# A written-out order of 1442 steps replaced by another one: linear attention and a gated MLP on one NeuronCore

## The chip, the cores and the metric

The kernel runs on one core of a Trainium2 chip. The metric is the device time of one execution in microseconds, as the median of several runs; smaller is better. The core has five engines that work side by side and wait for one another by semaphores: TensorE (PE in the profile, with PEld for its weight loads), VectorE (DVE), ScalarE (ACT), GpSimd (POOL) and SyncE (SP, which here only issues DMAs).

## The reference

The inputs are q, k, v and a complex decay a = a_re + i a_im, each of 4 batches x 8 heads x 768 positions x 48 channels, and four weight matrices. The first part is a linear attention with a decaying complex state per head; the second part is a gated MLP on the 3072 tokens of 384 features that come out of it.

```python
mag = sqrt(a_re**2 + a_im**2);  scale = minimum(mag, 0.999) / (mag + 1e-6)
for t in range(768):                       # state S is complex, 48 x 48 per head
    S = a[t] * S + outer(k[t], v[t])       # a[t] scaled as above, per row of S
    y[t] = q[t] @ real(S)
x = y as 3072 tokens x 384
g, val = x @ w_gate, x @ w_val             # 384 -> 1536
ffn = (gelu(g) * val) @ w_out              # 1536 -> 384
out = x + sigmoid(x @ w_res) * ffn
```

## The kernel before

**Tiling.** The sequence is cut into 6 chunks of 128 positions. One pair of a batch and a chunk is a unit, and `SIZES` (L19) groups the 24 units into 14 passes, numbered 0 to 13: passes 0 and 1 hold one unit each, passes 2 to 11 two units each, passes 12 and 13 one each. Within a chunk the attention is computed as matrix products; from chunk to chunk a state is carried (`Gf`, `Gb`).

**Steps.** The kernel does not issue instructions directly. The functions `prepare`, `attend` and `forward` (L373, L511 and below) are called for every pass and add steps to a plan: a step has an engine, a kind and a function that issues its instructions. There are 1442 steps. In this document a step is called by its pass and kind, for example `3.feat` or `1.gv`. The kinds that matter:

- `load` (SP): 120 transfers of 192 KB, for each unit ar, ai, q, k and vf. The weights are loaded from POOL's queue (`wgv`, `wr`, `wo`).
- `ln`, `exp`, `tai`, `sq`, `lnb`, `la`, `lh`, `ll`: logarithm of the decay's magnitude, split in a high and a low half; `cumL` (PE) sums it along the chunk and `pexpE`, `pexpI` (ACT) take exponentials. `mrd` is a small DMA of the last row, `mrc` a copy after it.
- `atan`, `carry` (a DMA that adds the last chunk's phase), `th`, `tl`, `cumT` (PE), `round` (ACT), `fr`, `abs`, `sin` (ACT): the phase, its running sum and its sine and cosine.
- `qe` and `feat` (DVE or POOL): features of q and k. They are transposed either on PE (`peT`, then a copy `cpT`; passes below `PE_T` = 6, L21) or by a DMA (`dT`, SP).
- `qk`, `am`, `av`, `kv`, `U`, `Gb`, `Gf`: the attention itself; `x` copies its result out of PSUM. `x` is transposed on PE (`peX`, `cpX`; passes below `PE_X` = 3, L20) or by a DMA (`dX`, SP).
- `gv` (PE, L605): the gate and value products, 12 steps of six matmuls for a pass; `gelu` (ACT, L610), `h` (DVE, L611), `res` (PE, L620) with `tanh` (ACT), `out` (PE, L631), `ot` (DVE), `otx` (DVE or POOL) and `store` (SP).

**Order.** `ORDER` (L43 to L106) is a list of all 1442 step numbers, written out by hand or by a program that is not part of the kernel. `Plan.run` (L161) walks through it and issues each step's instructions to its engine, so each engine executes its own steps in list order. An engine stops at an instruction whose inputs are not there, and everything behind it on that engine waits too. The list also sets three other things. A buffer goes to whichever of its copies is free first in the list: 8 PSUM banks, `WD` = 21 wide buffers (L22), `WH` = 8 half-wide ones and so on. The list decides where ScalarE changes its function table: a step carries a letter L (logarithm and exponential), T (arctangent and sine) or G (gelu and tanh), and whenever the letter differs from the last one a table load is issued:

```python
            if t.act is not None and t.act != table:
                table = t.act
                load(table)
```

The table load has line L647 in the profile. And it sets the turns of POOL and DVE: POOL's computing steps and DVE's steps of the kinds in `TWO_PORTS` (L24) are chained by an added wait whenever the turn passes from one engine to the other:

```python
            if t.port:
                if last is not None and last[0] != t.eng:
                    turn(ins, last[1])
                last = (t.eng, ins)
```

**Place.** Some steps can run on more than one engine. `place(default)` (L336) looks the step's number up in the dictionary `PLACE` (L29 to L42) and otherwise takes the default that its line names, for example `place("POOL")` for `vcast`, the cast of v to bf16.

Of the kernel before, what the change touches and what calls it, by code (L numbers as in the profile page):

```python
# [29 lines left out]
    23: "POOL", 24: "POOL", 35: "POOL", 40: "DVE", 50: "DVE", 51: "DVE", 53: "ACT", 64: "ACT", 105: "POOL", 114: "ACT",  # L30
    121: "DVE", 131: "DVE", 190: "DVE", 191: "POOL", 203: "ACT", 205: "ACT", 213: "DVE", 216: "POOL", 223: "DVE", 227: "DVE",
    230: "ACT", 252: "ACT", 285: "DVE", 291: "DVE", 305: "DVE", 306: "DVE", 333: "POOL", 334: "POOL", 338: "ACT", 340: "DVE",
    353: "DVE", 356: "POOL", 363: "DVE", 366: "POOL", 367: "DVE", 422: "DVE", 435: "ACT", 438: "POOL", 456: "DVE", 460: "DVE",
    472: "POOL", 482: "POOL", 518: "DVE", 524: "DVE", 551: "ACT", 554: "POOL", 555: "POOL", 562: "DVE", 565: "POOL",
    566: "POOL", 572: "DVE", 576: "DVE", 577: "DVE", 585: "DVE", 588: "POOL", 595: "DVE", 598: "POOL", 667: "DVE", 670: "POOL",
    671: "POOL", 681: "POOL", 682: "POOL", 691: "ACT", 700: "POOL", 710: "POOL", 746: "DVE", 767: "POOL", 779: "ACT",
    783: "POOL", 794: "POOL", 801: "ACT", 803: "ACT", 822: "POOL", 878: "DVE", 891: "ACT", 894: "POOL", 895: "POOL",
    905: "POOL", 924: "POOL", 931: "DVE", 934: "POOL", 970: "DVE", 976: "DVE", 1007: "POOL", 1017: "POOL", 1025: "ACT",
    1036: "POOL", 1042: "DVE", 1045: "POOL", 1113: "DVE", 1117: "POOL", 1124: "DVE", 1137: "ACT", 1152: "DVE", 1155: "POOL",
    1196: "DVE", 1210: "DVE", 1224: "POOL", 1225: "POOL", 1232: "DVE", 1243: "DVE", 1290: "DVE", 1296: "DVE", 1316: "ACT",  # L40
    1317: "POOL", 1325: "POOL", 1388: "ACT", 1389: "POOL", 1393: "DVE", 1397: "POOL", 1402: "DVE", 1440: "DVE",
}  # L42
ORDER = [  # L43
# [636 lines left out]
```

## Time and profile before

| | before |
|---|---|
| median of 3 runs | 262.19 us (261.19 to 263.16) |
| the profiled execution's own time | 262.64 us |
| its span, first to last instruction | 260.9 us |
| granted TensorE clock, mean | 0.98 |
| PE busy | 220.1 us (84%), 2362 matmuls |
| DVE busy | 211.2 us (81%), 372 instructions |
| ACT busy | 211.6 us (81%), 353 instructions, 36 of them table loads of 46.2 us in all |
| POOL busy | 118.8 us (46%), 138 instructions |
| transfers issued by SP | 192: 120 loads, 24 stores, 48 transposes |
| bytes moved | 41.92 MB, mean 161 GB/s |

How to read it: all times come from one profiled execution. The span ends 1.7 us short of that execution's own time. A matmul's record includes the time that it spends in the pipeline, so a PE that is busy for the whole of a stretch may still have room; the spacing from the start of one step to the start of the next tells more. Since every engine executes its part of the list in list order, the n-th step of an engine in the list is the n-th one of that engine in the trace, and each of the 1442 steps has a known start and end.

### The profile page before, as it was taken

Reading aid. Unit: us, or ns where it says so; the run is one execution under the profiler, and the core shown is the slowest. Engines: PE = TensorE matmul, PEld = TensorE weight load, DVE = VectorE, ACT = ScalarE, POOL = GpSimd, SP = SyncE. Lnnn points to the kernel's source line nnn. Section 1 sums busy time; section 2 is a strip of 40 time slices with the busy share of each in tenths; the row PEclk is TensorE's granted clock in tenths of the full one; section 3 lists DMA queues with packets and bytes.
Section 4 is the critical chain, followed back from the end, with each engine's and each line's share of the span. In section 5 each row is a group of like instructions: output and inputs, shape, how many; then the busy total and the mean of one; then the engine's idle time right before and its main releaser. Section 6 shows DMA issues by size and latency. Waiting matters only on the chain. (4 is left out here: it accounts for less than half of the span.)

```text
span 260.9 us, 6202 instructions
## 1 busy us (share of the span) xinstructions
PE 220.1 (84%) x2362; PEld 169.7 (65%) x2362; DVE 211.2 (81%) x372; ACT 211.6 (81%) x353; POOL 118.8 (46%) x138
## 2 busy tenths in 40 slices
PE   0220675799999999999999989999999989999993
PEld 0000333689878767786876767877878758876881
DVE  1476979789998989988888989888999866784463
ACT  4997979999999987999799979989988756931440
POOL 4225125869850687869435467644440510122101
PEclk9999995699999999999999999999999999999999
DMA  8999999996979999698997999999999976941221
GB/s 143 187 186 205 194 191 198 183 219 103 118 126 186 178 187 225 123 184 163 196 199 158 190 188 161 193 146 174 213 170 138 204 152 135 155 80 48 79 90 60
DMA packets 170621, 41.92 MB, mean 161 GB/s; under 512 B 164064, under 2 KB 170592, under 8 KB 170592
## 3 DMA queue, kind: packets, MB, share of 16 engines
q1 hardware_dynamic: 166144, 37.63, 85.3%
q0 software_dynamic: 4448, 3.90, 10.1%
q8 instruction: 18, 0.29, 0.5%
q14 instruction: 11, 0.09, 0.2%
HBM read 31.26 MB, written 4.72 MB: 138 GB/s over the span
## 5 line engine op out<-in xcount | busy, mean ns | idle before, releaser
L611 DVE SCALAR_TENSOR_TENSOR h<-h,pb 128x512 bf16<-128x512 bf16 (+1 forms) x84 | 48.9, 604 | 12.6 <-ACT h L610 6.8
L605 PE MATMUL pb<-xT,wv 128*128 128x256 bf16 (+1 forms) x504 | 57.6, 257 | 1.1 <-DVE h L611 0.9
L605 PE MATMUL pb<-xT,wg 128*128 128x256 bf16 (+1 forms) x504 | 56.3, 257 | 1.1 <-DMA xT<-x 0.9
L631 PE MATMUL pb<-wo,h 128*128 128x384 bf16 x288 | 55.1, 326 | 0.0
L610 ACT ACTIVATE h<-pb 128x512 bf16<-128x512 f32 (+1 forms) x84 | 41.6, 547 | 13.2 <-PE pb L605 12.6
L605 PEld LDWEIGHTS <-wg 128*128 128x128 bf16 x504 | 43.2, 98 | 7.9 <-DMA xT<-x 1.6
L605 PEld LDWEIGHTS <-wv 128*128 128x128 bf16 x504 | 43.1, 98 | 7.7 <-DMA xT<-x 1.1
L647 ACT ACT_TABLE_LOAD x36 | 46.2, 1283 | 1.3 <-PEq L664 0.7
L631 PEld LDWEIGHTS <-h 128*128 128x128 bf16 x288 | 26.4, 97 | 13.9
L537 DVE TENSOR_TENSOR am<-pb,mask 128x512 bf16<-128x512 f32 x48 | 31.9, 683 | 3.2 <-PE pb L534 2.9
L368 PEld LDWEIGHTS <-mask 128*128 128x128 bf16 x96 | 9.4, 107 | 23.5 <-issue 19.6
L638 POOL TENSOR_TENSOR ot<-ot,x 128x384 f32<-128x384 f32 x13 | 11.8, 909 | 19.7 <-DVE ot L635 18.1
L534 PE MATMUL pb<-QT,KT 96*128 96x128 bf16 x192 | 17.5, 225 | 2.6 <-DVE QT L343 1.4
L567 POOL TENSOR_TENSOR Gb<-U,M 96x384 bf16<-96x384 f32 x14 | 11.6, 827 | 17.7 <-DVE ll L418 4.2
L635 DVE SCALAR_TENSOR_TENSOR ot<-sg,pb 128x384 f32<-128x384 f32 x24 | 13.1, 547 | 6.9 <-ACT x L342 3.4
L406 POOL TENSOR_TENSOR t<-t,ai 128x768 f32<-128x768 f32 (+1 forms) x8 | 12.0, 1503 | 12.7 <-ACT t L404 8.1
L342 ACT CAST x<-pb 128x384 bf16<-128x384 f32 x17 | 8.0, 475 | 11.9 <-PE pb L548 8.7
L368 PE MATMUL pb<-th,mask 128*128 128x384 f16 x24 | 9.1, 378 | 10.0 <-DVE th L343 9.7
L534 PEld LDWEIGHTS <-KT 96*128 96x128 bf16 x192 | 13.4, 100 | 6.2 <-DMA KT<-fK 2.6
L481 POOL TENSOR_TENSOR Ke<-k,Ei 128x768 bf16<-128x768 f32 (+1 forms) x6 | 9.3, 1545 | 17.7 <-ACT Ei L427 9.3
L413 DVE SCALAR_TENSOR_TENSOR la<-s,la 128x768 f32<-128x768 f32 (+1 forms) x14 | 11.6, 836 | 6.4 <-ACT s L412 4.3
L620 PE MATMUL pb<-wr,xT 128*128 128x384 bf16 x72 | 15.3, 326 | 0.9 <-DMA xT<-x 0.9
(90 smaller groups left out, 463.5 us busy)
## 6 DMA issues: line engine op xcount, KB each, us to landing
ar<-in_a_re_dram SPq DMA_DIRECT2D x24, 192.0 KB, 4.6
ai<-in_a_im_dram SPq DMA_DIRECT2D x24, 192.0 KB, 4.7
k<-in_k_dram SPq DMA_DIRECT2D x24, 192.0 KB, 4.4
q<-in_q_dram SPq DMA_DIRECT2D x24, 192.0 KB, 4.2
vf<-in_v_dram SPq DMA_DIRECT2D x24, 192.0 KB, 4.1
out_dram<-ot SPq DMA_DIRECT2D x24, 192.0 KB, 2.5
wg<-in_moe_w_gate_dram POOLq DMA_DIRECT2D x6, 192.0 KB, 5.1
wv<-in_moe_w_val_dram POOLq DMA_DIRECT2D x6, 192.0 KB, 4.9
```

The lines of the kernel that those rows point to most:

```text
L368: nc.tensor.matmul(out=bank.tile, lhsT=mask[:, 0, :], rhs=x[:, i * DM:(i + 1) * DM], start=(j == 0), stop=(j == 1))
L406: add(e1, "tai", lambda: on[e1].tensor_tensor(out=F("t"), in0=F("t"), in1=flat(T("ai"), n), op=OP.mult), [s["ai"]], [s["t"]], n)
L534: nc.tensor.matmul(out=ap.tile[:, h, :], lhsT=kT.tile[0:DD, u * H // 2 + h, :], rhs=qT.tile[0:DD, u * H // 2 + h, :], start=True, stop=True)
L537: add("DVE", "am", lambda u=u, am=am, ap=ap: nc.vector.tensor_tensor(out=am.tile[:, u * H // 2:(u + 1) * H // 2, :], in0=ap.tile, in1=mask ...
L605: nc.tensor.matmul(out=o_.tile[:, u, :], lhsT=w_[:, k_, (2 * m + u) * 128:(2 * m + u + 1) * 128], rhs=s["xT"].tile[:, k_, 0:n].rearrange(" ...
L610: add("ACT", "gelu", lambda gp=gp, hv=hv: nc.scalar.activation(out=hv(), in_=gp.tile, func=AF.Gelu), [gp], [hh], n, "G")
L611: add("DVE", "h", lambda vp=vp, hv=hv: nc.vector.scalar_tensor_tensor(out=hv(), in0=hv(), scalar=0.5, in1=vp.tile, op0=OP.mult, op1=OP.mul ...
L620: nc.tensor.matmul(out=rp.tile, lhsT=s["xT"].tile[:, k_, i, :], rhs=wr[:, k_, :], start=(k_ == 0), stop=(k_ == KF - 1))
L631: nc.tensor.matmul(out=op_.tile, lhsT=s["h2"].tile[:, k_, i * 128:(i + 1) * 128], rhs=wo[:, k_, :], start=(k_ == 0), stop=(k_ == NF - 1))
L635: add("DVE", "ot", lambda i=i, op_=op_, ot=ot: nc.vector.scalar_tensor_tensor(out=ot.tile, in0=sg[i].tile, scalar=1.0, in1=op_.tile, op0=O ...
L638: add(e8, "otx", lambda i=i, ot=ot, e8=e8: on[e8].tensor_tensor(out=ot.tile, in0=ot.tile, in1=s["x"].tile[:, i].rearrange("p h d -> p (h d ...
L647: plan.run(ORDER, lambda table: nc.scalar.preload_act_table_set(ACT_SETS[table]), lambda ins, prev: tc.add_manual_dep(ins.ins, prev.ins.na ...
```

## The change

`PLACE` and `ORDER` are replaced, and nothing else. The steps, their dependencies, the sizes and the numbers of buffers are the same. The order is another throughout, and 85 steps run on another engine: 27 go from POOL to DVE, 22 from DVE to POOL, 13 from DVE to ACT, 9 from ACT to DVE, 9 from POOL to ACT and 5 from ACT to POOL. Walked through by `Plan.run`, the old list loads ScalarE's table 36 times and the new one 33 times. POOL has 118 steps in place of 127, ACT 325 in place of 317, DVE 368 in place of 367. By kind:

| engine | steps gained (net) | steps lost (net) |
|---|---|---|
| ACT | 4 `vcast`, 2 `th`, 2 `cpT`, 2 `Mc`, 1 `abs`, 1 `cpX`, 1 `x` | 4 `sq`, 1 `mrc` |
| DVE | 4 `sq`, 3 `tl`, 2 `Gb`, 2 `Gf`, 1 `th` | 2 `cpT`, 2 `Mc`, and one each of `qe`, `tai`, `x`, `vcast`, `abs`, `mrc`, `cpX` |
| POOL | 2 `mrc`, 1 `qe`, 1 `tai` | 3 `th`, 3 `tl`, 3 `vcast`, 2 `Gb`, 2 `Gf` |

The beginning of both (the rest of the list differs in the same manner):

```diff
 PLACE = {
-    23: "POOL", 24: "POOL", 35: "POOL", 40: "DVE", 50: "DVE", 51: "DVE", 53: "ACT", 64: "ACT", 105: "POOL", 114: "ACT",
-    121: "DVE", 131: "DVE", 190: "DVE", 191: "POOL", 203: "ACT", 205: "ACT", 213: "DVE", 216: "POOL", 223: "DVE", 227: "DVE",
+    23: "POOL", 24: "POOL", 33: "DVE", 44: "POOL", 53: "ACT", 64: "ACT", 105: "DVE", 114: "ACT", 117: "POOL", 121: "DVE",
+    145: "ACT", 190: "DVE", 191: "DVE", 203: "ACT", 213: "DVE", 223: "DVE", 227: "DVE", 228: "DVE", 230: "ACT", 252: "ACT",
...
 ORDER = [
-    16, 21, 17, 22, 97, 102, 103, 23, 24, 98, 104, 34, 105, 115, 116, 178, 117, 35, 118, 25, 179, 106, 188, 26, 27, 294, 36,
-    37, 293, 107, 108, 109, 295, 411, 110, 119, 120, 38, 28, 296, 303, 304, 111, 181, 29, 189, 410, 420, 121, 180, 305, 306,
+    16, 21, 97, 102, 98, 103, 104, 22, 105, 106, 17, 23, 24, 34, 295, 115, 35, 25, 116, 36, 107, 178, 108, 37, 294, 180, 117,
+    26, 293, 303, 179, 296, 38, 304, 181, 188, 109, 27, 118, 110, 111, 305, 119, 100, 28, 306, 189, 307, 29, 2, 30, 190, 191,
...
```

In words, for the parts that come up below: in the old list `1.sq` and `2.sq` run on POOL, in the new one on DVE; `0.abs` goes from DVE to ACT. The loads of pass 1's ar and ai stand second and third in place of third and fourth, pass 1's k stands 13th in place of 25th. ScalarE's steps ahead of its first G table come in seven groups in both lists: of 4, 2, 17, 8, 16, 8 and 11 steps before, of 5, 2, 12, 7, 19, 10 and 10 after. The last `ot`, `otx` and `store` belong to pass 13 before and to pass 12 after, on DVE and SP in both.

More of the change, by code (lines that the diff above doesn't have):

```diff
@@ L29 @@
 PLACE = {
-    23: "POOL", 24: "POOL", 35: "POOL", 40: "DVE", 50: "DVE", 51: "DVE", 53: "ACT", 64: "ACT", 105: "POOL", 114: "ACT",
-    121: "DVE", 131: "DVE", 190: "DVE", 191: "POOL", 203: "ACT", 205: "ACT", 213: "DVE", 216: "POOL", 223: "DVE", 227: "DVE",
-    230: "ACT", 252: "ACT", 285: "DVE", 291: "DVE", 305: "DVE", 306: "DVE", 333: "POOL", 334: "POOL", 338: "ACT", 340: "DVE",
-    353: "DVE", 356: "POOL", 363: "DVE", 366: "POOL", 367: "DVE", 422: "DVE", 435: "ACT", 438: "POOL", 456: "DVE", 460: "DVE",
@@ L34 @@
[L34 to L38, printed above, removed]
@@ L39 @@
-    1036: "POOL", 1042: "DVE", 1045: "POOL", 1113: "DVE", 1117: "POOL", 1124: "DVE", 1137: "ACT", 1152: "DVE", 1155: "POOL",
-    1196: "DVE", 1210: "DVE", 1224: "POOL", 1225: "POOL", 1232: "DVE", 1243: "DVE", 1290: "DVE", 1296: "DVE", 1316: "ACT",
-    1317: "POOL", 1325: "POOL", 1388: "ACT", 1389: "POOL", 1393: "DVE", 1397: "POOL", 1402: "DVE", 1440: "DVE",
+    23: "POOL", 24: "POOL", 33: "DVE", 44: "POOL", 53: "ACT", 64: "ACT", 105: "DVE", 114: "ACT", 117: "POOL", 121: "DVE",
+    145: "ACT", 190: "DVE", 191: "DVE", 203: "ACT", 213: "DVE", 223: "DVE", 227: "DVE", 228: "DVE", 230: "ACT", 252: "ACT",
@@ new lines @@
+    291: "DVE", 305: "DVE", 306: "DVE", 333: "POOL", 345: "ACT", 347: "ACT", 353: "DVE", 357: "DVE", 363: "DVE", 366: "POOL",
+    408: "DVE", 422: "DVE", 423: "DVE", 438: "POOL", 446: "DVE", 456: "DVE", 460: "DVE", 469: "DVE", 472: "POOL", 482: "POOL",
+    518: "DVE", 539: "DVE", 551: "ACT", 554: "ACT", 562: "DVE", 565: "POOL", 566: "POOL", 572: "DVE", 576: "DVE", 577: "DVE",
+    579: "ACT", 588: "POOL", 595: "DVE", 598: "POOL", 670: "ACT", 671: "POOL", 681: "POOL", 682: "POOL", 689: "ACT",
@@ new lines @@
+    691: "ACT", 700: "POOL", 710: "POOL", 711: "DVE", 752: "DVE", 767: "POOL", 783: "POOL", 794: "POOL", 801: "ACT",
+    803: "ACT", 812: "POOL", 822: "POOL", 823: "DVE", 858: "DVE", 894: "ACT", 902: "DVE", 905: "POOL", 913: "ACT", 924: "POOL",
+    991: "POOL", 1003: "ACT", 1006: "POOL", 1017: "POOL", 1025: "ACT", 1042: "DVE", 1045: "POOL", 1080: "DVE", 1086: "DVE",
+    1101: "POOL", 1113: "ACT", 1116: "POOL", 1117: "POOL", 1135: "ACT", 1137: "ACT", 1146: "POOL", 1190: "DVE", 1196: "DVE",
+    1210: "DVE", 1224: "ACT", 1225: "POOL", 1235: "POOL", 1236: "POOL", 1255: "DVE", 1296: "DVE", 1325: "POOL", 1330: "DVE",
@@ L42 @@
+    1368: "DVE", 1388: "ACT", 1389: "POOL", 1393: "DVE", 1396: "POOL",
 }
 ORDER = [
[62 rows of a table removed]
[63 rows of a table added]
 ]
```

121 rows, old and new, of the table ORDER are left out of this document.

## The prediction

> **What bounds the kernel now.** I looked first at the page's slices: who is busy when.
>
> ```profile
> PE   0220675799999999999999989999999989999993
> ...
> DVE  1476979789998989988888989888999866784463
> ACT  4997979999999987999799979989988756931440
> POOL 4225125869850687869435467644440510122101
> ```
>
> Three regimes: up to about 52 us PE is half empty while ACT and DVE work; then all three are full; from about 200 us ACT and DVE thin out and only PE is full. The chain that ended last says the same of the end: from 214.65 us on it is almost only PE.
>
> ```profile
> 221.51 7.86 PE pb L605 x72
> ...
> 244.51 6.70 PE pb L605 x120
> ```
>
> These lines give PE's real pace: six matmuls, one `gv` step, take 0.655 us with two units (7.86/12) and 0.335 us with one (6.70/20). In the same way `out` takes 0.650, `res` 0.488, a `cumL` or `cumT` 0.325, `qk` 0.225, `peT` 0.448, `av` 0.406, `kv` 0.205 us from start to start. With 120 and 48 `gv`, 72 `out`, 24 `res`, 48 sums, 48 `qk`, 20 `peT`, 20 `av`, 20 `kv` and 4.5 us of small ones this is 205.2 us, the same before and after. PE's first step starts at 9.7 us, its last ends at 256.4, so it loses 256.4 - 205.2 = 51.2 us; behind it come `ot`, `otx` and the last store, 4.5 us. **So the time is 205.2 + what PE loses + 4.5.** The first `gv` starts at 52.3 us with 10.6 us of PE work done: 41.7 us are lost in the start and 9.5 after it. By 60 us 42.8 are lost, so 8.4 in the last 200 us.
>
> Next, what feeds PE. I set each engine's steps one after the other at their start-to-start times (`gelu` 0.49, `h` 0.60, `feat` 0.87 and so on), and called the rest idle. At 60 us ACT has idled 9.4 and DVE 18.7; at 200 us 21.6 and 32.9, against 49.1 for PE. So between 60 and 200 us ACT idles 12.2, DVE 14.2, PE 6.3 of 140 us: PE bounds, the other two are close. In the start it is the reverse: ACT idles 4.3 us from 20 to 60 us, PE 23.9. There ACT's list sets the pace, with waits such as these, of ACT and DVE in the first 60 us:
>
> ```profile
> ACT CS L475 <- DVE fw L471: 1.1, 1, 1.1
> ACT fr L460 <- PE pb L368: 1.0, 3, 0.5
> ACT Ei L427 <- PE pb L368: 0.8, 1, 0.8
> ...
> ACT mr L342 <- DMA mr<-E: 0.5, 1, 0.5
> ```
> ```profile
> DVE la L413 <- ACT s L412: 4.3, 2, 3.2
> ```
>
> **The change, part by part.** *Engine sums.* The costs come from rows like these, by shape:
>
> ```profile
> L647 ACT ACT_TABLE_LOAD x36 | 46.2, 1283 | 1.3 <-PEq L664 0.7
> ...
> L409 ACT ACTIVATE s<-t 128x768 f32<-128x768 f32 x7 | 5.9, 842 | 0.0
> ...
> L411 POOL TENSOR_TENSOR s<-t 128x768 f32<-128x768 f32 x2 | 2.9, 1460 | 2.0 <-DVE t L406 1.9
> ...
> L342 ACT CAST v<-vf 128x768 bf16<-128x768 f32 x2 | 1.7, 840 | 0.0
> ```
>
> Three table loads less are 3 x 1.283 = 3.85 us. ACT gets 4.66 us of steps net: four `vcast` 2.9, two `cpT` 1.8, `th` 1.65, four small kinds 1.35, four `sq` away -2.9, `mrc` -0.1. So ACT has 0.8 us *more* to do. DVE gets 3.7 us more (`sq` 3.1, `tl` 2.6, `Gb` and `Gf` 1.9, less 3.9 for the rest), POOL 9.0 less. The saved tables do not show in PE's 205.2; in the tail, where ACT is 55% idle, nothing of this counts. What counts is the start and whether PE is fed in the middle.
>
> The Trainium skill, in ScalarE: Activation LUTs, section Terms, puts a table load at about 2.7 us. By it three loads would be 8.1 us and ACT 3.4 us lighter; the row's 1283 ns decides.
>
> *Start.* ACT's own work ahead of its first G step is 46.8 us before (first `gelu` at 55.9, so 9.1 us idle) and 46.7 after. Walking the new list with the same durations and the landing times of loads of the same rank: the wait of 1.1 us for `0.abs` goes, as ACT does it itself; the 0.5 us for pass 1's `mrc` goes, as it stands later; `2.lnb` can start at 18.5 instead of 20.8, as `2.sq` no longer waits for POOL. One wait comes: `0.cpT` on ACT needs the transpose that PE has queued behind `1.kv`, and that needs pass 1's v, load 28 in place of 23 (28.2 us before, some 33 to 35 now), about 1.1 us. This gives 6.5 us of idle if every step hits its row; the old trace has some 1.7 us of small losses beyond its listed waits, so 8.2, and I take 8.0. `1.cpX` then ends at 43.9 + 0.4 + 8.0 = 52.3 us, and PE's dense part begins with `1.res` at 52.4 with 11.2 us done: 41.2 us lost, 0.5 better.
>
> DVE has 39.9 us ahead of its first `h` before (58.3 us) and **46.4** after. Its 3.2 us wait at `2.la` goes, and at that point it has idled 10.4 instead of 13.9. Then `3.th` waits about 0.8 for its carry, `am` 0.5, and `4.fr` about 1 for `4.round`, which ACT has three microseconds later in its list: 12.5 to 14 at the first `h`, 13.3 in the middle. So the first `h` comes at 59.7, when PE's list has 18.0 us ahead of it (15.9 before): PE has lost 41.7 there, against 42.8. **Sum: -1.1 us.**
>
> *Middle.* Read at equal PE positions, the new list holds 5 us more DVE work ahead from 20 us of PE work to 180 (+5.4, +5.2 at 60, +4.9 at 100, +4.2 at 180) and 1 to 3 us more of ACT's. The five are those it did in the start's idle time. DVE idles 10% of the middle either way, mostly in pieces below 1 us, so I let PE lose the same 8.4 us after 60. If that cover is gone the price is the 5 us. SP's list has each transpose within a few ranks of its old place, and its long wait for `3.x` (17.5 us, ended at 72.8 by DVE) ends some 2 us sooner. Nothing between 60 and 256 us is free for POOL's 9 us: its idle time is already half the span.
>
> *End.* The last `out` is followed by `ot` and `otx` on DVE and the store in both lists: 4.5 us again.
>
> **The sum.** 262.64 is the profiled execution's own time, 1.7 over its span and 0.45 over the median of 262.19. 262.64 - 1.1 - 0.45 = **261.1 us**. What a measurement can tell here is about 1%: 259.6 and 264.8 are the bounds of "same".
>
> **Rivals.**
> - *The start's lead is kept whole* (0.25). If no small losses come, ACT has idled 6.5 us, PE starts dense at 50.7 with 39.5 lost (-2.2), and the earlier SP queue halves PE's gaps ahead of steps that need a DMA transpose (1.05, 0.97, 1.10, 1.06 and two of 0.3, together 4.8; I take off 1.9 in place of 2.4, as not all wait for that alone): **258.1**. For it: the waits named are real; against: DVE's first `h` holds PE back to 41.
> - *DVE becomes the bound* (0.23, slower). It has 5 us more ahead of every `gv`, and PSUM banks come free only by `h`. If the 3.2 us wait at `2.la` is replaced by another (a carry, a q or k that lands late), the first `h` comes after 62 us and PE cannot catch up: up to +5, I take +4.5: **266.7**. It decides from 62 us on; at 60 or less it is off. For it: DVE is 92% busy from 60 to 200 us; against: 14.2 us idle there.
> - *Transposes come too late* (0.13). In the list `6.dX` stands straight ahead of pass 6's first `gv`, 5.7 us of PE work ahead before; `7.dT` 1.0 (7.7), `11.dT` 1.3 to 2.8 (7 to 10). They take 3.3 to 3.9 us to land, so these three could cost 3.4 + 2.7 + 2.4, less what is lost there now: about +4, **265.1**. It needs SP to issue them as late as the list stands; SP runs by its own queue, whose ranks hardly differ.
> - *PE goes into its dense part at half clock* (0.05). From 40 to 50 us the granted clock is 0.50 and a `peT` takes 0.83 us; from 50 to 55 us its mean is 0.98, so it came back at about 50.2 us, 4.2 us after PE's steps had closed up (46.0). If another pattern just ahead of the dense part puts such a 4.2 us stretch inside it, half of it is lost: +2.1, **263.2**. The Trainium skill, in TensorE: Matmul & The Clock Gate, section What's actually happening, has full clock after about 3.4 us of sustained work; the trace agrees in kind.
> - *The change is no change* is inside the forecast: 262.2.
>
> **Chances and range.** Forecast 261.1: 0.34, itself 259 to 264.8. Faster by over 1%: the first rival 0.25 and 0.03 of the forecast, 0.28. Slower: DVE 0.23, transposes 0.10, 0.02 of the forecast, 0.35. Same: 0.37. Lead and loss are both likely, so the range takes in most of the first rival and of the second: 257.2 to 267.0.
>
> **What would show it.** 33 table loads; ACT's first G step near 54.7 and not after 56; DVE's first `h` at 59 to 60.5, its wait at `2.la` below 0.5; PE's losses 41 to 42 at the first dense step and 8 to 9 after 60 us; no PE gap above 1.5 us at passes 6, 7 and 11. It is wrong if DVE idles less than 10 us between 60 and 200 us while PE loses more than 10 there, or if the start is won by 2 us or more.

## The result

| | before | changed kernel |
|---|---|---|
| median of 20 runs each, run beside one another | 261.10 us (260.01 to 263.16) | 259.99 us (257.95 to 262.01) |
| ratio of the two | | 0.9947, 95% interval 0.9923 to 0.9970 |
| the profiled execution's own time; its span | 262.64; 260.9 us | 259.86; 258.1 us |
| last PE step ends; the rest of the span | 256.4; 4.5 us | 254.0; 4.1 us |
| PE's loss at 60, 70, 140, 200 us and at the end | 42.8, 42.9, 45.8, 49.1, 51.2 us | 44.3, 45.2, 48.1, 48.4, 48.7 us |
| ScalarE's table loads | 36 | 33 |

The change is worth half a per cent, and the interval is clear of 1. The ratio compares means and leaves out one run of the changed kernel that fell in a slower state (262.01 us); the two medians alone would give 0.9957. "PE's loss" is the prediction's measure: the time up to which PE has come less the start-to-start work that it has done by then. The frame holds: 205.2 + 48.7 + 4.1 = 258.0 us is the new span, and 1.8 us more is the execution's own time. The two profiled executions differ by 2.8 us, twice what the 20 runs show, since the one of before took 1.5 us more than the median of its kernel. What is read from these two traces below therefore shows where time is lost; its sizes are those of two executions.

First the slices of the changed kernel: who is busy when, in 40 parts of the span.

```profile
PE   0132864769999999999789999999999999999993
...
DVE  2499888997999999998988989889998967866363
ACT  5899869989999999999969989999999498331440
POOL 1424145437452395948816386716105514210011
```

The three regimes are as they were: half-empty PE up to some 52 us, everything full until about 200 us, then PE alone. The chain that ended last shows the same end (columns: start, length, what):

```profile
217.47 9.17 PE pb L606 x84
...
240.11 2.01 PE pb L606 x36
```

These are 9.17/14 = 0.655 us for a `gv` step of two units and 2.01/6 = 0.335 us for one of one unit: PE's pace is exactly the old one, so all of the difference is in what PE waits for. Of the engines' groups, the changed ones read as forecast:

```profile
L648 ACT ACT_TABLE_LOAD x33 | 42.3, 1283 | 1.3 <-PEq L665 0.7
...
L410 ACT ACTIVATE s<-t 128x768 f32<-128x768 f32 x3 | 2.5, 842 | 0.0
```

Now the start, by the waits of ACT in the first 60 us and of DVE in the first 64 us (total, times, longest):

```profile
ACT KT L343 <- PE pb L504: 2.8, 3, 2.1
ACT la L404 <- DMA ar<-in_a_re_dram: 2.4, 2, 1.5
ACT s L413 <- DVE s L412: 1.4, 3, 0.9
```
```profile
DVE t L407 <- ACT t L405: 3.4, 1, 3.4
DVE th L344 <- ACT t L437: 2.6, 1, 2.6
DVE tl L455 <- POOL t L407: 1.4, 1, 1.4
...
DVE am L538 <- PE pb L535: 1.1, 1, 1.1
```

The old 3.2 us wait at `2.la` and the 1.1 us wait of ACT for `0.abs` are gone. The wait of `0.cpT` for its transpose has come, 2.1 us long, and DVE has a wait that the prediction did not have: `tl` for POOL's `t`. This is `5.tl` waiting for `6.tai`, and not for its data but for its turn. It stands in DVE's timeline right ahead of the first `h` (start, length; the bracket is the idle time before):

```profile
59.69 0.96 DVE L455 TENSOR_TENSOR tl<-t,th 128x768 bf16<-128x768 f32 x1 [1.45 <-POOL t L407]
...
62.57 0.74 DVE L612 SCALAR_TENSOR_TENSOR h<-h,pb 128x256 bf16<-128x256 bf16 x2
```

So DVE's first `h` comes at 62.57 us. It came at 58.33 us before, and 59.7 was forecast. PE's loss by 70 us is 2.3 us *larger* than before, not 1.1 smaller.

The gain is in the middle, where PE loses 48.7 - 45.2 = 3.5 us after 70 us instead of 51.2 - 42.9 = 8.3. By the table all of it comes after 140 us: between 70 and 140 us PE loses 2.9 us in both, and from there to the end 5.4 us before and 0.6 after. PE's longest waits from 75 to 256 us, of the kernel before and then of the changed one:

```profile
PE pb L534 <- DMA KT<-fK: 1.1, 3, 0.8
PE pb L503 <- DVE fQ L486: 1.0, 2, 0.6
PE pb L605 <- DMA xT<-x: 0.9, 1, 0.9
PE pb L620 <- DMA xT<-x: 0.9, 1, 0.9
PE pb L605 <- DVE h L611: 0.9, 1, 0.9
```
```profile
PE pb L535 <- DMA KT<-fK: 1.5, 1, 1.5
PE pb L606 <- DMA xT<-x: 0.6, 1, 0.6
```

`KT<-fK` and `xT<-x` are the DMA transposes `dT` and `dX`. The row that names `h` is one of them too: it is the wait of `5.gv` at 124.26 us, where that `h` had ended 1.6 us earlier and the transpose of `5.x` landed at 124.12. No row ends on ScalarE. A row counts from the end of the last matmul's record; from start to start six gaps before make 4.8 us (`5.gv` 1.05, `7.qk` 0.97, `8.gv` 1.10, `10.res` 1.06 and two of 0.3 at `11.qk`), and two are left after: `5.gv` 0.73 and `6.qk` 1.66. Also gone are the 1.3 us before `4.peT` and `5.peT` (waits for `feat`).

### The profile page after: what moved, and what is told of

Read it like the earlier page. It is cut to its first block, busy times and chain, and to the rows that moved or that the text cites. A ratio compares the mean times of both kernels' runs of the same rounds, so it can differ in the third digit from the quotient of the medians.

```text
span 258.1 us, 6191 instructions
## 1 busy us (share of the span) xinstructions
PE 219.4 (85%) x2362; PEld 171.2 (66%) x2362; DVE 214.4 (83%) x373; ACT 210.4 (82%) x358; POOL 109.7 (42%) x129
## 4 chain that ended last, share of the span: by engine, by line
PE 59%; DVE 11%; DMA 9%; issue 7%; POOL 6%; SPq 4%; ACT 2%; DVEq 0%; POOLq 0%
PE pb L606 29%; PE pb L632 15%; PE pb L621 4%; SPq L383 4%; PE pb L369 3%; DVE h L612 3%; PE pb L535 3%; DMA q<-in_q_dram 2%; POOL t L407 2%; DMA mr<-E 2%; DMA KT<-fK 2%; DMA ai<-in_a_im_dram 2%; DMA t<-fr 2%; PE pb L547 1%; PE pb L504 1%
## 5 line engine op out<-in xcount | busy, mean ns | idle before, releaser
L606 PE MATMUL pb<-xT,wg 128*128 128x256 bf16 (+1 forms) x504 | 57.0, 257 | 1.3 <-ACT sg L623 0.9
L606 PE MATMUL pb<-xT,wv 128*128 128x256 bf16 (+1 forms) x504 | 56.8, 257 | 0.6 <-DMA xT<-x 0.6
L612 DVE SCALAR_TENSOR_TENSOR h<-h,pb 128x512 bf16<-128x512 bf16 (+1 forms) x84 | 48.5, 603 | 10.4 <-ACT h L611 5.8
L632 PE MATMUL pb<-wo,h 128*128 128x384 bf16 x288 | 53.5, 326 | 0.0
L535 PE MATMUL pb<-QT,KT 96*128 96x128 bf16 x192 | 18.5, 226 | 2.9 <-DMA KT<-fK 1.5
L407 POOL TENSOR_TENSOR t<-t,ai 128x768 f32<-128x768 f32 (+1 forms) x9 | 13.8, 1542 | 11.0 <-DVE s L412 5.4
L535 PEld LDWEIGHTS <-KT 96*128 96x128 bf16 x192 | 14.1, 101 | 6.7 <-DMA KT<-fK 1.8
L568 POOL TENSOR_TENSOR Gb<-U,M 96x384 bf16<-96x384 f32 x12 | 9.9, 823 | 15.6 <-DVE fQ L487 7.0
L573 POOL TENSOR_TENSOR Gf<-U,M 96x384 f32<-96x384 f32 x9 | 7.5, 828 | 19.4 <-DVE tl L455 7.1
L463 DVE SCALAR_TENSOR_TENSOR fr<-fr,pb 128x384 f32<-128x384 int32 x24 | 12.8, 545 | 2.2 <-ACT fr L461 2.2
L369 PE MATMUL pb<-lh,mask 128*128 128x384 f16 x24 | 9.1, 380 | 5.7 <-DVE lh L417 5.7
```

The lines of the kernel that those rows point to most:

```text
L369: nc.tensor.matmul(out=bank.tile, lhsT=mask[:, 0, :], rhs=x[:, i * DM:(i + 1) * DM], start=(j == 0), stop=(j == 1))
L407: add(e1, "tai", lambda: on[e1].tensor_tensor(out=F("t"), in0=F("t"), in1=flat(T("ai"), n), op=OP.mult), [s["ai"]], [s["t"]], n)
L463: add("DVE", "fr", lambda i=i: nc.vector.scalar_tensor_tensor(out=T("fr")[:, i], in0=T("fr")[:, i].bitcast(INT), scalar=-TWO_PI, in1=cth[i ...
L535: nc.tensor.matmul(out=ap.tile[:, h, :], lhsT=kT.tile[0:DD, u * H // 2 + h, :], rhs=qT.tile[0:DD, u * H // 2 + h, :], start=True, stop=True)
L606: nc.tensor.matmul(out=o_.tile[:, u, :], lhsT=w_[:, k_, (2 * m + u) * 128:(2 * m + u + 1) * 128], rhs=s["xT"].tile[:, k_, 0:n].rearrange(" ...
L612: add("DVE", "h", lambda vp=vp, hv=hv: nc.vector.scalar_tensor_tensor(out=hv(), in0=hv(), scalar=0.5, in1=vp.tile, op0=OP.mult, op1=OP.mul ...
```

## Experiments

All ratios are to the kernel before, run on the same chip beside the experiment; the chip and its level differ a little between the groups of runs, so ratios are compared and not times. A trace is one execution: the five traces with the new list up to 70 us have lost 44.8 to 46.5 us there, the three with the old list 42.9 to 43.9. So a difference of less than about 1.5 us between two traces says little by itself. The rivals after the result: **adding up** (a microsecond that PE loses in the start stays to the end, and one won in the middle too) against **given back** (the start's loss vanishes later), and, for the middle, **transposes** against **table loads**.

### Order and places apart

The new order with the old engine choices, and the old order with the new ones:

```diff
 PLACE = {
-    (the new dictionary)
+    (the old dictionary)
 ORDER = [
     (the new list)
```
```diff
 PLACE = {
-    (the old dictionary)
+    (the new dictionary)
 ORDER = [
     (the old list)
```

> The new list with the old choice of engines: every step stands where the change puts it, but runs on the engine of before. Theory A (the order carries the change, the engines hardly matter): 260.0 us, ratio to before 0.995, PE loses 44 to 45 us by 60 us and 3 to 5 after. Theory B (order and engines belong together, since a step's place in the list was chosen for its duration on its engine, and POOL's long steps hold DVE's turn): slower than both kernels, 263 to 267 us, with waits of DVE for POOL's turn above 1 us. POOL has 9.0 us more to do than in the new kernel, DVE 3.7 less.

> The old list with the new choice of engines. Theory A (the order carries the change): 261.1 us, ratio 1.00. Theory C (the engines carry it, POOL's 9 us less on the turn between POOL and DVE): 260 us or less, ratio 0.995. Theory B (they belong together): 263 to 267 us.

Measured: 293.1 us, ratio 1.1169 (1.1110 to 1.1227), and 297.1 us, 1.1338 (1.1288 to 1.1388). The direction was expected, the size was not: 30 us. The busy sums of DVE, ACT and POOL hardly move (212, 208 and 118 us in the first), but PE loses 81.0 and 84.3 us. A part of that is PE's clock, which was granted at 0.50 for 17.1 us after 60 us in the first and for 6.8 us in the second (not at all in the two kernels); as an estimate, half of these stretches, up to 8.6 and 3.4 us. For the rest, look at DVE's waits for POOL. These are the longest of the first experiment:

```profile
DVE fK L597 <- POOL Ke L592: 4.0, 2, 2.9
DVE th L454 <- POOL th L454: 4.0, 1, 4.0
DVE fQ L597 <- POOL Qe L592: 3.7, 1, 3.7
DVE ot L749 <- POOL ot L749: 2.7, 1, 2.7
```

The `th` that waits for a `th` is `1.th` behind `0.th`, the `ot` that waits for an `ot` is `4.otx` behind `3.otx`: no data passes between them, only the turn. The `fK` and `fQ` rows are data, `feat` waiting for its own `qe`, late on a POOL that waited for turns itself. All rows "DVE ... <- POOL" add up to 9.2 us in the kernel before and 7.8 in the changed one, but 33.6 and 30.0 in these two. Each list is laid out so that POOL's steps and DVE's two-port steps come in runs; 85 steps on the wrong engine break the runs up. No run takes the turns out, so how much of the 30 us is theirs is not shown. But neither half of the change has a price of its own. They can only be taken together.

### The start and the rest apart

A cut through the list does work: the first 360 steps as in one list with its places, the rest in the order and with the places of the other.

```diff
-ORDER = [ (new list) ]
+ORDER = [ (old list's first 360 steps), (the others, in the new list's order) ]
```
```diff
-ORDER = [ (old list) ]
+ORDER = [ (new list's first 360 steps), (the others, in the old list's order) ]
```

> The first 360 steps of the old list (up to about 70 us), then the rest in the order of the new one, each step on the engine that its list gives it. Theory M1 (the new list's middle feeds PE better by itself, 3.4 to 4.1 us lost after 60 us in place of 8.1, and the start is a separate loss of 1.5 to 2.3 us): the old start's 42.9 us lost at 70 us, then 3.5 to 4.5: 257.5 to 258.5 us, ratio 0.986 to 0.990. Theory M3 (the new middle loses less only because PE comes into it 2 us later, while DMA keeps its own calendar: what the start lost is given back): PE's waits for transposes come back, 5 to 8 us lost after 70 us, and 260 to 261 us, ratio 0.995 to 1.00.

> The first 360 steps of the new list, then the rest in the order of the old one. Theory M1: the new start's 45.2 us lost at 70 us and the old middle's 8: 263 to 263.5 us, ratio 1.008 to 1.010. Theory M3 (what the start loses is given back by shorter waits later): 260.5 to 261.5 us, ratio about 1.00, PE loses 5 to 6 us after 70 us.

Measured: old start with new rest 260.4 us, 0.9950 (0.9913 to 0.9986), with 33 table loads; new start with old rest 262.6 us, 1.0029 (0.9998 to 1.0060), with 36. With the changed kernel's 0.9947 this is a table of four. Replacing the rest is worth 0.5 points with the old start and 0.8 with the new one, 1.3 to 2.1 us: the gain of the change is here. Replacing the start costs 0.3 points (0.8 us) ahead of the old rest and nothing ahead of the new one, though ahead of the new rest PE has lost 43.9 us at 70 us with the old start and 45.2 with the new one. Of that lead of 1.3 us 0.7 is left at the end (48.0 against 48.7), and both are within the spread of traces. Ahead of the old rest PE loses 50.1 - 44.8 = 5.3 us after 70 us, as "given back" had it. The first `h` is at 57.9 us in one and at 62.6 us in the other, at the same time in all: a late first `h` did not decide. "Given back" is nearer for the new rest; for the old one the interval leaves both open.

### The middle: transposes

In the old list alone, 13 of the DMA transposes were issued one or two places earlier on SP; in the new list ten, one to four places earlier.

```diff
 ORDER = [  # old list, SP's part
-    ..., (a load or a store), (5.dX1), ...
+    ..., (5.dX1), (a load or a store), ...
```

> The old list with the old places; only 13 of the transposes by DMA (dX and dT of passes 5 to 11: those that waited over 0.8 us on SP with their source ready and landed less than 3 us before PE took them) are issued one or two places earlier on SP, ahead of the loads or stores that stood before them. In the trace of before six of PE's gaps in the middle are waits for such transposes, 4.8 us together; in the changed kernel's trace two are left, 2.4 us. Theory A (the middle's gain of the changed kernel is the place of its transposes on SP): PE's gaps for dX and dT shrink to 2 to 3 us, and the time falls by 1 to 2.5 us, 0.990 to 0.996 of before. Theory B (the gaps come from elsewhere: what starts later is waited for elsewhere, because the rest of the old list is laid out for these waits): gaps of the same sum at other steps, 0.997 to 1.004.

> The new list with the new places; ten transposes by DMA that waited on SP with their source ready are issued one to four places earlier. Theory A: the two gaps that are left (0.73 us before 5.gv, 1.66 us before 6.qk) go, at most 2.4 us, and the time falls to 0.986 to 0.991 of before. Theory B: the time stays at 0.993 to 0.998 of before, within 0.8 us of the changed kernel, or rises because the loads that are moved behind come later.

Measured: old list 261.3 us, 0.9969 (0.9945 to 0.9993); new list 261.5 us, 0.9975 (0.9948 to 1.0002). On the old list it is a gain of 0.3 points, of the size of half of the change's gain, with PE's loss at the end 50.4 instead of 51.2. Its gaps for transposes fell from 4.8 to 2.1 us, but 0.70 us before `7.res` and 1.08 before `8.res`, both for banks, are new. On the new list it is no gain, rather 0.3 points worse than unmoved: the 1.66 us before `6.qk` did go, and came back as 0.60 before `6.gv`, 0.60 before `4.peT` and pieces. So the place of the transposes can be *part* of what the new list gained; on the new list nothing more was won by it.

### The middle: table loads

Three loads of the table that is there already, ahead of one `gelu` each of passes 4, 6 and 8:

```diff
+            if j in (508, 720, 948):
+                load(t.act)
             ins = t.fn()
```

> The new list with three more loads of ScalarE's table, 36 as before: the same G table again ahead of one gelu step of pass 4, one of pass 6 and one of pass 8 (near 113, 144 and 184 us). They add 3 x 1.283 = 3.85 us to ACT and change nothing else. Theory that ACT's load is covered (the prediction's): 0 to 0.8 us over the changed kernel, 0.994 to 0.998 of before, with ACT's idle time smaller by what the loads take. Rival, that the three loads saved are the gain: each is on the path, +3 to +3.85 us, 1.006 to 1.010 of before.

Measured: 262.6 us, 0.9999 (0.9972 to 1.0025): the whole gain of the change is gone. Against the changed kernel it is 0.52 points, 1.4 us, between the two theories; the two intervals together allow 0.4 to 2.3. The traces agree: from 70 us to the end PE loses 51.7 - 46.5 = 5.2 us instead of 3.5. (The 46.5 us, 1.3 more than in the changed kernel, were lost ahead of the first of the three: PE's granted clock was 0.50 from 58.1 to 61.5 us.) ACT's timeline around the first of them (each line one group of instructions):

```profile
113.41 0.60 ACT L612 ACTIVATE h<-pb 128x512 bf16<-128x512 f32 x1
113.90 0.84 ACT L471 ACTIVATE fw<-fr 128x768 f32<-128x768 f32 x1
114.63 0.59 ACT L612 ACTIVATE h<-pb 128x512 bf16<-128x512 f32 x1
115.24 1.28 ACT L649 ACT_TABLE_LOAD   x1
116.53 1.08 ACT L612 ACTIVATE h<-pb 128x512 bf16<-128x512 f32 x2
117.51 0.21 ACT L344 COPY mr<-mr 16x48 f32<-16x48 f32 x1
```

ACT does not wait anywhere here, so `5.mrc`, the copy in the last line, comes a load later, and PE's `5.M` waits 1.0 us for it, a wait that the changed kernel does not have. Another 0.9 us stands at `6.gv`, for the bank that `6.gelu` frees behind the second load. The three loads therefore cost about a third of their 3 x 1.283 us, not nothing, and not all.

### Taking away two loads more

If three loads cost 1.4 us, two fewer should bring 0.9. `7.lnb` has an L group to itself and moves into the next one with the `la` that follows it; `6.gelu4` has a G group to itself and moves into the one before, with its `gv` step.

```diff
 ORDER = [
-    ..., (7.lnb), ..., (7.la), ..., (5.pexpI), ..., (6.gv8), ..., (6.gelu4), ...
+    ..., (5.pexpI), (7.lnb), (7.la), ..., (6.gv3), (6.gv8), (6.gelu2), (6.gelu4), ...
```

> The new list with two steps moved: 3.M (PE) and 3.Mc (ACT) stand six PE steps later, behind 1.gv8, so that PE does not stand 1.08 us at 57 us for the cast on POOL that 3.M reads; their users stand over 40 steps later. Theory that what PE loses in the start stays in the time: the gap goes, PE has lost about 1 us less at 70 us, and the time falls by 0.7 to 1.1 us, to 0.990 to 0.993 of before. Rival, that PE's loss in the start is given back, because the feature chain on DVE (first h at 62.6 us) sets the pace of what follows: the gap goes but the time stays within 0.4 us of the changed kernel, 0.993 to 0.997 of before.

> The new list with two loads of ScalarE's table less, 31 in place of 33, and nothing else moved but what that takes: 7.lnb, which stands alone in an L group near 78.5 us, goes into the next L group (near 93.5 us) with the la that follows it; 6.gv8 and its gelu, which has a G group of its own near 157.8 us, go into the G group before (6.gv8 behind 6.gv3, near 145 us). In the run with three loads more the time rose by 1.4 us against the changed kernel, that is 0.45 us for each load of 1.283 us. If the loads are worth the same when they go: 0.9 us less than the changed kernel, 0.990 to 0.993 of before, and PE has lost 0.5 to 1.5 us less at 180 us. Rival, that the three loads more cost only because they stood right ahead of a gelu that PE waits for, and other loads are covered: 0.993 to 0.997 of before.

> The same 31 loads, and 3.M and 3.Mc six PE steps later as in the run that moved them alone (0.9931 of before). If both edits add: 0.988 to 0.991 of before, the fastest list of this study. If they overlap: 0.991 to 0.995.

Measured: `3.M` later 260.2 us, 0.9931 (0.9900 to 0.9961); 31 loads 266.3 us, **1.0094** (1.0056 to 1.0132); both 265.9 us, 1.0112 (1.0084 to 1.0140). The first brought PE's wait for `3.mrc` from 0.92 us to nothing, but PE's loss at 70 us stayed (45.7), with 0.79 us new at `2.av`: given back at once. The second is 1.5 points slower than the list it came from, and both theories had it faster or equal; so had those for the two edits together. POOL's timeline of the 31 loads shows where it begins:

```profile
90.67 0.21 POOL L343 COPY mr<-mr 16x48 f32<-16x48 f32 x1
95.75 0.83 POOL L572 TENSOR_TENSOR Gf<-U,M 96x384 f32<-96x384 f32 x1 [4.87 <-DVE la L413]
```

In the changed kernel the same two lines stand right behind each other:

```profile
90.64 0.21 POOL L344 COPY mr<-mr 16x48 f32<-16x48 f32 x1
90.82 0.82 POOL L573 TENSOR_TENSOR Gf<-U,M 96x384 f32<-96x384 f32 x1
```

And this follows from it in the 31 loads, on DVE and on PE:

```profile
103.40 0.96 DVE L486 TENSOR_TENSOR fK<-Ke,CS 128x1536 bf16<-128x1536 bf16 x1 [3.08 <-POOL Ke L481]
```
```profile
105.01 0.34 PE L520 MATMUL pb<-idf,mr 16*96 16x16 f32 x2 [2.27 <-DVE am L537]
```

`7.la` is a DVE step of a two-port kind. Put in the middle of a run of nine steps of POOL it takes the turn twice: POOL's `3.Gf` must wait for `7.la`, which stands behind a queue of DVE's own steps and waits for `7.lnb` on ACT. POOL stands 4.9 us, everything behind it there comes 4.6 us later, DVE stands 3.1 us at `5.feat` for `5.qe`, and behind `5.feat` stands `4.am`, whose bank `4.M` needs. PE has lost 50.9 us at 140 us instead of 48.1. A step that takes 0.95 us wherever it stands, moved to save a load of 1.3 us, cost 2.8.

The test of this reading keeps the turn: in the list with `3.M` later, `7.lnb` moves into the next L group, and its `la` to where DVE has the turn already.

```diff
 ORDER = [
-    ..., (7.lnb), ..., (7.la), ..., (9.exp), ..., (5.vcast), (7.lh), ...
+    ..., (9.exp), (7.lnb), ..., (5.vcast), (7.la), (7.lh), ...
```

> The list with 3.M and 3.Mc six PE steps later (0.9931 of before), and one load less, 32: 7.lnb goes out of its L group of its own into the next one, behind 9.exp (near 102 us). Its la stands behind 5.vcast, where DVE has POOL's turn already (near 113 us), and not in the middle of a run of POOL's steps as in the two runs with 31 loads: there POOL stood 4.9 us for it (90.9 to 95.8 us), DVE 3.1 us for 5.qe and PE 2.4 us for the bank of 4.am. Theory that the turn was what made those two runs slow: no such stop of POOL, 4.M waits less than 0.5 us, PE's loss at 140 us is within 1 us of the changed kernel's 48.1, and the time is 0.988 to 0.994 of before. Rival, that ACT's own steps in another grouping make it slow, or a wide buffer held longer: PE has lost 1.5 us or more over the changed kernel at 140 us, 0.997 or more.

Measured: 260.6 us, 0.9969 (0.9944 to 0.9994). POOL's run is whole again:

```profile
90.73 0.21 POOL L343 COPY mr<-mr 16x48 f32<-16x48 f32 x1
90.90 0.82 POOL L572 TENSOR_TENSOR Gf<-U,M 96x384 f32<-96x384 f32 x1
```

Between 70 and 140 us PE loses 47.1 - 44.7 = 2.4 us, against 5.7 in the 31 loads and 2.9 in the changed kernel, and nothing is seen at `4.M`: the turn was the cause up to there. Of what follows in the 31 loads (2.5 us more lost between 140 and 180 us, where ACT waits 1.3 us for the earlier `6.gv8`) this run says nothing, as it leaves that edit out. And the load saved is not seen in the time. By 180 us PE has lost 49.3, with 0.80 us at `7.gv` for a bank that `6.ot` frees late. None of these lists is shown to beat the changed kernel. The one with `3.M` later is level with it within the intervals.

### How much of it is DMA

The prediction had ACT's list set the pace of the start. Loads that read long rows tell this from the arrival of the data:

```diff
-in_=src[b, :, c * 128:(c + 1) * 128, :].rearrange("h t d -> t h d")
+in_=src[b].rearrange("h t d -> (h t) d")[c * 1024:(c + 1) * 1024, :].rearrange("(p h) d -> p h d", h=H)
```

> The new list unchanged; each of the 120 loads of ar, ai, q, k and v reads its 192 KB as 128 rows of 1536 bytes that lie one after the other, in place of 1024 rows of 192 bytes. The loads then hold other positions and heads than the reference wants, so all results are computed from wrongly placed inputs; the number of bytes, the steps, their shapes and their order are the same. It tells what in the start and in the middle is DMA. Theory that ACT's list sets the pace of the start (the prediction's): the loads land earlier, but PE's loss at the first dense step falls by less than 2 us, and the time to no less than 0.985 of before. Rival, that the arrival of the loads sets it: the first loads land in half of the time, PE's loss at its first dense step falls by 5 us or more, and the time to 0.965 to 0.98. In the middle, the two gaps that wait for transposes (0.73 and 1.66 us) shrink if the transposes are late because the loads crowd the DMA engines, and stay if they are late because they stand behind others on SP.

Measured: 257.1 us, 0.9754 (0.9708 to 0.9799); by the profiled executions 257.36 against 259.86 us. The first 60 us of SP's queue, packets, MB and share of the 16 engines' time, of the changed kernel and then with long rows:

```profile
q1 hardware_dynamic: 47840, 9.05, 91.1%
```
```profile
q1 hardware_dynamic: 6624, 9.05, 47.7%
```

The DMA engines' share halves, and a load of `ar` lands after 4.2 instead of 4.7 us there. PE's first dense step comes 1.2 us sooner (51.5), where the rival had 5 us or more. At 60 us PE has lost 44.4 us, as with short rows (44.3), but here its granted clock was 0.50 from 56.2 to 59.6 us, inside the dense part, and four `gv` steps there took 1.3 us longer; with short rows it was 1.00. So the start gains about a microsecond at most: ACT's list sets it in the main, as the prediction had it. In the middle it is the other way: after 70 us PE loses 46.2 - 45.0 = 1.2 us instead of 3.5, the transposes' two gaps are gone, and the trace lists no wait of PE from 75 to 256 us. So with half of the loads' work off the DMA engines the transposes come in time from the same places in SP's queue: from source ready to issue it is 0.4 us in the median instead of 1.1. The time fell further than the 0.985 that this theory allowed, since it had counted the start alone. By the ratios it is 1.9 points against the changed kernel. The two traces show only 1.0%, but they are of two chips (the kernel before took 262.9 us beside this run, 261.1 beside the changed kernel), and only this one has the half clock in the dense part.

The Trainium skill, in DMA: Bandwidth & Descriptors, section Specifications, gives 512 bytes as the least transfer for full rate. The trace agrees in kind: the same 9.05 MB took 91.1% of the engines' time in rows of 192 bytes and 47.7% in rows of 1536.

## Why the prediction was right, and where it was not

The time (261.1 us against 262.19) was a gain of 0.42%; measured is 0.53%. But the two terms behind it were both wrong, with opposite signs: by the traces the start was 2.6 us worse than forecast and the middle 4.0 us better. That the sum came so near is luck.

- **Frame.** Right: PE's pace and the end (4.1 for 4.5 us) are as they were, and all that changed is PE's loss.
- **Start, first half.** Right: ACT's first G step at 55.1 us (54.7), PE's first dense step at 52.7 (52.4) with 41.5 us lost (41.2), DVE's idle time at `2.la` 10.4 us as worked out, its wait there gone. The new wait of `0.cpT` was 2.1 us instead of 1.1.
- **Start, DVE's first `h`: the first term mis-sized.** "12.5 to 14 at the first `h`, 13.3 in the middle" was 16.2 us, and 59.7 was 62.6. The walk had followed data and left out the turns between POOL and DVE: `5.tl` waited 1.45 us for `6.tai`, which stood on POOL behind `3.mrc`, and `3.mrc` had waited 3.7 us for its DMA. It also had 0.5 for `am` where 1.1 came, and no wait for `0.cpT` on DVE (0.7). "-1.1 us" was +1.5 at 60 us and +2.3 at 70. PE's own gaps up to 60 us, which make that loss, end elsewhere: 1.05 before `0.gv` on the bank that `1.tanh` frees behind ACT's table load, 1.08 before `3.M` on `3.mrc`, 0.59 before `0.gv` on the bank of `3.cpT` on ACT. The walk had none of the three. That the late `h` itself cost PE time is not shown.
- **Middle: the second term mis-sized.** "I let PE lose the same 8.4 us after 60" was 48.7 - 44.3 = 4.4 us. The transposes' gaps halved, from 4.8 to 2.4 us, which the prediction had only in the rival that keeps the start's lead (1.9 us). It had the cause there as an SP queue that runs earlier; SP's queue did not run earlier there (its 105th transfer is issued at 135.6 us before and 136.5 after). The transposes stand better in it: from source ready to issue is 2.4 us in the median before, 1.1 after. The experiments put 0.3 points on their place in the old list and 0.5 on three table loads. Together these are of the right size, but they were measured at other places than those of the change, so how the gain splits is not shown. For the transposes speaks that the gaps that went after 140 us were nearly all theirs (3.8 us).
- **"The saved tables do not show."** Not so for every place: three loads put into the middle cost some 1.4 us (0.4 to 2.3), though ACT idles 11.4 us between 60 and 200 us. ACT has 0.8 us more of work in all, as forecast (its steps are 162.9 instead of 158.2 us from start to start, its loads 3.85 us less). Of the three loads saved two fell between 140 and 200 us and one later. Whether they are worth as much there is not shown: the run with one load less and the turn kept was no faster.
- **Rival "DVE becomes the bound".** Its condition came true, first `h` after 62 us; its price of 4.5 us did not. The deciding point was wrong: with the first `h` at 57.9 or 62.6 us the time is the same. DVE idled 27.8 - 16.2 = 11.6 us between 60 and 200 us, PE lost 4.1 there, so DVE did not bound.
- **Rival "the start's lead is kept".** Its condition failed: PE's dense part began at 52.7 us and not at 50.7. Its other half, the transposes' gaps halved, came true without it.
- **Rival "transposes too late".** `6.dX`, `7.dT` and `11.dT`, which it named, did not come late. One gap above 1.5 us at pass 6 did come, from `6.dT` (1.66).
- **Rival "half clock".** The granted clock of the traced execution was 1.00 up to its end, so its condition did not come. Two other runs with the same start show what it is worth. With 0.50 from 36.1 to 49.7 us, ahead of the dense part (the 31 loads), PE has lost the same 44.3 us at 60 and 45.2 at 70. With 0.50 from 58.1 to 61.5 us, inside it (the three more loads), it has lost 1.3 us more at 70. The rival's half of the stretch would be 1.7.
- **What the forecast could not see** is how close both lists stand to something much slower. Half of the change alone costs 12 to 13%, and the rivals reached 2%.

## What to carry to other kernels

When a written order shares one resource between two engines by turns, walk the turns as well as the data: a step on the wrong side of a run of the other engine's steps costs the whole queue in front of it, 4.9 us for a step of 0.95 us here. An order and its engine choices are one object; test pieces cut *along* the order, not one without the other. And a loss in an early stage need not reach the end: ask at each later stage whether the feeding engine has that much idle time left, and read PE's loss at several times, and in more than one execution, rather than one gap.

## What was not expected of the hardware

Rows of 192 bytes in place of 1536 take nearly twice the DMA engines' time for the same bytes (91.1% against 47.7% of the first 60 us), yet a load lands only 0.5 us (ar) to 1.3 us (k, v) later there. What the long rows helped was mostly the middle, where the transposes share the queue, and little the start. And a ScalarE table load that reloads the same table takes the full 1.28 us.
